# Decoding float64 weights in a fused kernel: a new order of steps, the remainder on VectorE, a third decode buffer

## The chip, the cores and the metric

One core of a Trainium2 chip runs the whole program. The metric is device time of one execution in microseconds (us), lower is better. Engines are named as the profile names them: PE is TensorE's matmuls, PEld its weight loads, DVE is VectorE, ACT ScalarE, POOL GpSimd, SP SyncE, whose queue issues most transfers. Each engine runs its own instructions strictly in the order in which the program emits them, and waits on semaphores for the others.

## The reference

Three parts, each feeding the next: a recurrent linear attention, a mixture of 8 experts with one expert per token, and a gated MLP over the 1536 tokens. The last part, with weights of 384 x 1536, 384 x 1536 and 1536 x 384, is what the diff is about:

```python
def _moe2_ref(x, w_gate, w_val, w_out) -> np.ndarray:
    gate = 1.0 / (1.0 + np.exp(-(x @ w_gate)))
    val = x @ w_val
    return (gate * val @ w_out).astype(np.float32)
...
h = np.maximum(np.einsum('ecd,edf->ecf', disp, w1), 0.0)
y = np.einsum('ecf,efd->ecd', h, w2)
```

The gated MLP's weights reach the kernel as float64 numbers (1536 x 384 of them in each of three matrices).

## The kernel before, in words

**Split products.** Every operand of a product is kept as a pair: a rounded part (`fp32r`) and the remainder that the rounding leaves. A product of two pairs is three matmuls: high by high, and the two cross terms. So each weight tile of 128 x 768 needs a copy that rounds it (ScalarE) and a subtraction that leaves the remainder (VectorE or GpSimd).

**Decoding.** The MLP's weights come as 18 tiles of 128 x 768 float64, read as pairs of 32-bit integers (`r64`, 768 KB a tile, two buffers). `decode(n)` returns a list of steps for tile n. Step o1 (L157) makes a float32 exponent and mantissa from the high word on ScalarE with Abs and a scale, into a work tile `wf`; o2 (L160) clamps it, o3 (L163) shifts it, o4 (L167) puts in the sign and o5 (L171) the low bits, all on VectorE; o6 rounds it into its home on ScalarE (L177) and subtracts on GpSimd (L178) for the remainder; o7 fetches the tile that comes two later in `ORDER` (L149), into the `r64` buffer that o5 has just read for the last time. Tiles 0 to 11 hold the gate and value weights of one block f of 128 columns each, tiles 12 to 17 the output weights of two blocks.

**Where decoding stands.** The first EARLY = 7 tiles of `ORDER` are decoded while the experts run: the expert loop has 64 iterations and 4 more, each with 9 matmuls of the first layer (`s1`), 9 of the second (`s2`, four iterations behind), and pieces of other work emitted behind them. Among these are `bg` (it rounds and subtracts one weight tile of the experts: copy L137, subtraction L139 on VectorE in even iterations and on GpSimd in odd ones, and a `raw` load on SP's queue 8 tiles ahead, which waits for its buffer), scatters of token ids by GpSimd (L190, iterations 4 to 15), `eload` (the load of an expert's tokens into `xr`, L795, in iteration f = 5 of the expert two before; TensorE transposes it at L804 in f = 1 and f = 4 of the expert before), and from iteration 6 on one step of decoding per iteration. So a tile takes seven iterations: the six steps with work, and o7.

**The MLP.** The tokens are four strips j of 384. For a strip and a block f, `mf` makes two tiles `pg` in PSUM (gate and value, 18 matmuls), `gate` makes of them the sigmoid `sg` (ScalarE), the product `gg` (VectorE), its rounded part `gh` (ScalarE) and the remainder `gl` (VectorE), and `mo` multiplies that with the output weights (9 matmuls). Two lanes of strips alternate, the second SKEW = 2 behind; `pg` is one buffer each, so the next `mf` needs `sg` done for its first half and `gg` for its second, while a `mo` of an older gate runs between two `mf`. The other 11 tiles are decoded here, one tile in each k of the loop, steps o1 to o3 ahead of the first lane's gate, o4 and o5 behind its `mo`, o6 and o7 behind the second lane.

**What sets the order.** It is written out by hand: the order of emission is the order on each engine. The lines touched are `ORDER`, `decode`, the list `dops` of the early tiles, the MLP's loop over k, and two allocations that make room for the third `wf`. The emission in the MLP's loop, shortened:

```python
for k in range(24 + SKEW):
    ops = decode(todo.pop(0)) if todo else []
    ...                                    # ops[:3]
    gate(*lane(0, k), mf(*lane(0, k)))
    mo(*lane(0, k - 1))
    ...                                    # ops[3:5]
    gate(*lane(1, b), mf(*lane(1, b)))     # b = k - SKEW
    mo(*lane(1, b - 1))
    ...                                    # ops[5:]
```

Of the kernel before, what the change touches and what calls it, by code (L numbers as in the profile page):

```python
# [7 lines left out]
F32 = mybir.dt.float32  # L8
F32R = mybir.dt.float32r
BF16 = mybir.dt.bfloat16  # L10
I32 = mybir.dt.int32
# [22 lines left out]
WARM = 16  # L34
BG = (0, 0, 0, 0, 0, 0, 4, 3)
DP = 2
ORDER = (0, 1, 2, 12, 3, 4, 13, 5, 6, 14, 7, 8, 15, 9, 10, 16, 11, 17)
EARLY = 7
HPB = 4
OVP = 60  # L40
# [62 lines left out]
def body(tc, A, out):  # L103
    nc = tc.nc
    E = mybir.EngineType
    with ExitStack() as top, tc.manual_schedule():
        gp_ = top.enter_context(tc.tile_pool(name="gp", bufs=1))
# [36 lines left out]
        r64, wyh, wyl = {}, {}, {}  # L144
        spl, homes = [None], []

        def dfetch(n):
            r64[n] = spl[0].tile([128, 768, 2], I32, tag="r64", name="r64", bufs=2)
            nc.sync.dma_start(out=r64[n].rearrange("p a b -> p (a b)"), in_=wy[n])  # L149

        def decode(n):
            t = {}

            def o1():
                t["a"] = spl[0].tile([128, 768], F32, tag="wf", name="wf", bufs=2)
                t["i"] = t["a"].bitcast(I32)
                nc.scalar.activation(out=t["a"], in_=r64[n][:, :, 1].bitcast(F32), func=AF.Abs, scale=2.0 ** 16)  # L157

            def o2():
                nc.vector.tensor_scalar(out=t["a"], in0=t["a"], scalar1=2.0, scalar2=DMAX, op0=ALU.max, op1=ALU.min)  # L160

            def o3():
                nc.vector.tensor_scalar(out=t["i"], in0=t["i"], scalar1=4, scalar2=1, op0=ALU.logical_shift_left,  # L163
                                        op1=ALU.logical_shift_right)

            def o4():
                nc.vector.scalar_tensor_tensor(out=t["i"], in0=r64[n][:, :, 1], scalar=-2 ** 31, in1=t["i"],  # L167
                                               op0=ALU.bitwise_and, op1=ALU.bitwise_or)

            def o5():  # L170
                nc.vector.scalar_tensor_tensor(out=t["i"], in0=r64[n][:, :, 0], scalar=29, in1=t["i"],  # L171
                                               op0=ALU.logical_shift_right, op1=ALU.bitwise_or)
                r64.pop(n)

            def o6():
                wyh[n], wyl[n] = homes.pop(0)
                nc.scalar.copy(out=wyh[n], in_=t["a"])  # L177
                nc.gpsimd.tensor_sub(wyl[n], t["a"], wyh[n].bitcast(F32))  # L178

            def o7():  # L180
                k = ORDER.index(n)
                if k + 2 < 18:
                    dfetch(ORDER[k + 2])

            return [o1, o2, o3, o4, o5, o6, o7]

        scx, sci = [], []

# [14 lines left out]


        rt = top.enter_context(tc.tile_pool(name="rt", bufs=2))
        tri = gp_.tile([128, 128], BF16, tag="tri", name="tri")
        ones = gp_.tile([128, 128], BF16, tag="ones", name="ones")
        warm = gp_.tile([1, 8], F32, tag="warm", name="warm")
        capi = gp_.tile([128, 1], I32, tag="capi", name="capi")
# [11 lines left out]
        with ExitStack() as ctx:  # L221
            xp_ = ctx.enter_context(tc.tile_pool(name="xsp", bufs=2))
            cp = ctx.enter_context(tc.tile_pool(name="ac", bufs=1))
# [5 lines left out]
            urow = cat[:, 128:512]  # L229
            rev = cat[:, 768:776]  # L230
            iw = cat[:, 776:1320].rearrange("p (a x) -> p a x", x=136)
            wd = cp.tile([112, 4], F32, tag="wd", name="wd")
            pw = cp.tile([112, 8, 3, 4], F32, tag="pw", name="pw")
            ft = cp.tile([112, 2, 4, 128], F32, tag="ft", name="ft")
# [459 lines left out]
        with ExitStack() as ctx:  # L694
# [18 lines left out]
            def overflow():  # L713
                with tc.If(offv["most"] > 256):
                    if True:
                        tb = rt.tile([1, 4, 40], F32, tag="tb", name="tb", bufs=1)
                        ti = rt.tile([1, 4, 40], I32, tag="ti", name="ti", bufs=1)
                        nb = cf[0:1, :].unsqueeze(2).to_broadcast([1, 8, 5])
                        ob = off[0:1, :].unsqueeze(2).to_broadcast([1, 8, 5])

                        def row(q):
                            return tb[:, q, :].rearrange("o (e j) -> o e j", j=5)

                        def con(q):
                            return cst[0:1, 128 + 40 * q:168 + 40 * q].rearrange("o (e j) -> o e j", j=5)

                        nc.vector.tensor_sub(row(0), nb, con(0))
                        nc.vector.tensor_scalar_add(row(1), nb, -256.0)
                        nc.vector.tensor_tensor(out=row(1), in0=row(1), in1=con(0), op=ALU.min)
                        nc.vector.tensor_add(row(2), row(1), ob)  # L730
                        nc.vector.tensor_add(row(1), row(1), con(1))
                        nc.vector.tensor_copy(out=row(3), in_=con(2))
                        nc.vector.tensor_scalar_max(tb, tb, 0.0)
                        nc.vector.tensor_copy(out=ti, in_=tb)
                        with tc.For_i(0, 40, 1) as i:
                            more = nc.values_load(ti[0:1, 0, bass.ds(i, 1)], min_val=0, max_val=1536,
                                                  skip_runtime_bounds_check_because="at most every token")
                            with tc.If(more > 0):
                                r0 = nc.values_load(ti[0:1, 1, bass.ds(i, 1)], engines=[E.SP], min_val=0,
                                                    max_val=8 * 1536 - 256,  # L740
                                                    skip_runtime_bounds_check_because="inside an expert's rows")
                                c0 = nc.values_load(ti[0:1, 2, bass.ds(i, 1)], engines=[E.DVE], min_val=0,
                                                    max_val=1536,
                                                    skip_runtime_bounds_check_because="inside the tokens")
                                w0 = nc.values_load(ti[0:1, 3, bass.ds(i, 1)], engines=[E.SP], min_val=0,
                                                    max_val=28,
                                                    skip_runtime_bounds_check_because="four times an expert's index")
                                block(r0, c0, w0)
# [44 lines left out]
            def eload(e, eng=nc.sync):  # L793
                xr[e] = mp.tile([128, 2, 384], F32, tag="xr", name="xr")
                after(eng.dma_start(out=xr[e], in_=xs_d[e * 1536:e * 1536 + 256, :].rearrange("(b p) d -> p b d", p=128)), scx)  # L795
# [59 lines left out]
                nc.vector.tensor_sub(XL[m][:, d], ys[e][m], XH[m][:, d].bitcast(F32))  # L855

            xt[0] = (xeh, xel)
            dops = [op for n in ORDER[:EARLY] for op in decode(n)]
            dops.reverse()
            fetch(sum(BG) + FIRST)  # L860
            eload(1)
            dfetch(ORDER[0])
            dfetch(ORDER[1])
            seq = [(e, f) for e in range(8) for f in range(8)]
# [47 lines left out]
        with ExitStack() as ctx:  # L912
# [26 lines left out]
            def gate(j, f, pg):  # L939
                sg = qp.tile([128, 384], F32, tag="sg", name="sg")  # L940
                nc.scalar.activation(out=sg, in_=pg[0], func=AF.Sigmoid)  # L941
                gg = qp.tile([128, 384], F32, tag="gg", name="gg")
                nc.vector.tensor_mul(gg, sg, pg[1])  # L943
                gh = qp.tile([128, 384], F32R, tag="gh", name="gh", bufs=7)
                gl = qp.tile([128, 384], F32R, tag="gl", name="gl", bufs=7)
                nc.scalar.copy(out=gh, in_=gg)  # L946
                nc.vector.tensor_sub(gl, gg, gh.bitcast(F32))  # L947
                gs[(j, f)] = (gh, gl)
# [21 lines left out]
            def lane(first, k):  # L970
                return (first + 2 * (k // 12), k % 12)

            todo = list(ORDER[EARLY:])
            for k in range(24 + SKEW):
                ops = decode(todo.pop(0)) if todo else []
                for op in ops[:3]:
                    op()
                if k < 24:
                    gate(*lane(0, k), mf(*lane(0, k)))
                if 0 < k <= 24:  # L980
                    mo(*lane(0, k - 1))
                for op in ops[3:5]:
                    op()
                b = k - SKEW
                if b >= 0:
                    gate(*lane(1, b), mf(*lane(1, b)))
                if 0 < b <= 23:
                    mo(*lane(1, b - 1), (0, 1, 2) if b < 20 else (0, 1) if b < 22 else (0,))
                for op in ops[5:]:
                    op()  # L990
            for f, t in ((7, 2), (8, 2), (9, 2), (9, 1), (11, 0), (10, 1), (11, 1), (10, 2), (11, 2)):
                mo(3, f, (t,))

# [16 lines left out]
```

## Time and profile before

| | |
|---|---|
| three runs | 479.15, 480.61, 486.78 us; median 480.61 |
| profiled execution | 480.61 us, of which the span of its instructions is 478.9 us |
| mean granted clock of TensorE | 0.977 |
| PE busy | 446.5 us, 93% of the span |
| DVE, ACT, POOL busy | 280.6, 220.8, 184.5 us |
| first matmul of the MLP | 241.62 us from the span's start |

The profile shows one execution. Times in its views count from the start of the span. A matmul's end is modelled, so successive matmuls overlap in it. "x <- y L9" after an idle time names what ended it and the line that issued that. The granted clock is 1.00 at 2.4 GHz and 0.50 at 1.2 GHz; a value between is a stretch with both.

### The profile page before, as it was taken

What the parts mean: (1) busy time and instruction counts of PE and PEld (TensorE: products, weight loads), DVE (VectorE), ACT (ScalarE), POOL (GpSimd) and SP (SyncE); (2) the same over time, 40 slices, a digit from 0 to 9 for tenths busy, and PEclk for the clock granted to TensorE, in tenths of its full rate; (3) what the DMA queues carried; (4) which work ended last, traced back from release to release, by engine and by line L of the source; (5) the groups of instructions that cost most, each with busy time, mean ns of one, the idle gap of its engine ahead of it and who ended that gap; (6) DMA issues with size and microseconds to landing.
All of it is one profiled execution on the core that took longest, in us unless ns stands there. A gap on an engine that the chain in (4) does not pass through costs nothing.

```text
span 478.9 us, 8621 instructions
## 1 busy us (share of the span) xinstructions
PE 446.5 (93%) x3354; PEld 431.4 (90%) x3356; DVE 280.6 (59%) x474; ACT 220.8 (46%) x450; POOL 184.5 (39%) x127
## 2 busy tenths in 40 slices
PE   6978988599979999999989899999999999999995
PEld 2777987599979999999979799999999999999995
DVE  4797997668778788889347676566222221212221
ACT  2676877536736777675332433433232322222231
POOL 4876938735885647467111311221120200000022
PEclk9979999799989999999999999999999999999999
DMA  7999951779898787773012312310010100000011
GB/s 213 347 340 309 273 203 72 248 288 216 197 227 305 269 271 238 254 258 101 3 47 86 133 66 75 124 68 0 1 49 1 49 1 0 1 1 0 1 50 49
DMA packets 23707, 65.10 MB, mean 136 GB/s; under 512 B 4592, under 2 KB 8816, under 8 KB 23664
## 3 DMA queue, kind: packets, MB, share of 16 engines
q1 hardware_dynamic: 21600, 59.80, 40.5%
q0 software_dynamic: 1920, 4.73, 2.7%
q8 instruction: 27, 0.44, 0.4%
q14 instruction: 16, 0.13, 0.1%
q10 hardware_dynamic: 144, 0.00, 0.0%
HBM read 56.65 MB, written 7.87 MB: 135 GB/s over the span
## 4 chain that ended last, share of the span: by engine, by line
PE 44%; DVE 3%; issue 3%; ACT 1%; POOL 1%; POOLq 0%; DVEq 0%; ACTq 0%
PE pg L936 28%; PE po L960 5%; PE po L959 5%; PE po L958 5%; DVE wf L160 1%; PE ph L825 1%; PE py L848 1%; DVE gg L943 1%; POOL out_dram L190 1%; PE py L849 1%; PE py L850 1%; DVE wf L167 1%; ACT wf L157 1%; DVE wf L171 0%; DVE gl L947 0%
## 5 line engine op out<-in xcount | busy, mean ns | idle before, releaser
L943 DVE TENSOR_TENSOR gg<-sg,pg 128x384 f32<-128x384 f32 x48 | 26.5, 553 | 93.6 <-PE pg L936 91.6
L139 POOL TENSOR_TENSOR rl<-raw,rh 128x768 fp32r<-128x768 f32 x26 | 52.1, 2006 | 36.0 <-ACT rh L137 35.9
L936 PE MATMUL pg<-xhi,ws 128*128 128x384 f32 x240 | 61.6, 337 | 4.6 <-ACT sg L941 3.0
L946 ACT CAST gh<-gg 128x384 fp32r<-128x384 f32 x48 | 24.7, 514 | 83.9 <-DVE gg L943 83.9
L190 POOL DMA_INDIRECT out_dram<-ob,ids x12 | 11.7, 976 | 123.8 <-ACT ob L967 121.4
L941 ACT ACTIVATE sg<-pg 128x384 f32<-128x384 f32 x48 | 23.5, 490 | 70.6 <-PE pg L936 70.6
L848 PE MATMUL py<-hh,rh 128*128 128x256 f32 x192 | 54.6, 284 | 0.0
L137 ACT CAST rh<-raw 128x768 fp32r<-128x768 f32 x64 | 51.4, 836 | 4.7 <-PE py L849 1.9
L849 PE MATMUL py<-hl,rh 128*128 128x256 f32 x192 | 53.5, 279 | 0.0
L850 PE MATMUL py<-hh,rl 128*128 128x256 f32 x192 | 53.5, 278 | 0.0
L139 DVE TENSOR_TENSOR rl<-raw,rh 128x768 fp32r<-128x768 f32 x31 | 46.3, 1497 | 10.6 <-ACT rh L137 10.5
L936 PE MATMUL pg<-xlo,rh 128*128 128x384 f32 x144 | 48.7, 338 | 0.0
L936 PE MATMUL pg<-xhi,rh 128*128 128x384 f32 x144 | 48.6, 338 | 0.0
L936 PEld LDWEIGHTS pg<-xhi,ws 128*128 128x128 f32 x240 | 43.0, 188 | 6.1 <-ACT sg L941 3.7
L936 PE MATMUL pg<-xhi,rl 128*128 128x384 f32 x144 | 48.5, 337 | 0.0
L947 DVE TENSOR_TENSOR gl<-gg,gh 128x384 fp32r<-128x384 f32 x48 | 26.8, 558 | 27.8 <-ACT gh L946 27.8
L936 PE MATMUL pg<-xlo,ws 128*128 128x384 f32 x120 | 40.2, 335 | 0.0
L178 POOL TENSOR_TENSOR rl<-wf,rh 128x768 fp32r<-128x768 f32 x8 | 14.7, 1840 | 65.4 <-ACT rh L177 59.9
L848 PEld LDWEIGHTS py<-hh,rh 128*128 128x128 f32 x192 | 36.4, 189 | 0.1
L850 PEld LDWEIGHTS py<-hh,rl 128*128 128x128 f32 x192 | 36.5, 190 | 0.0
L849 PEld LDWEIGHTS py<-hl,rh 128*128 128x128 f32 x192 | 36.5, 190 | 0.0
L327 ACT ACTIVATE at<-cst,dl 128x128 f32<-128x128 f32 x96 | 28.9, 387 | 7.6 <-DVE dl L319 7.5
(187 smaller groups left out, 1211.9 us busy)
## 6 DMA issues: line engine op xcount, KB each, us to landing
raw<-in_wx_dram SPq DMA_DIRECT2D x64, 384.0 KB, 5.6
r<-in_wy_dram SPq DMA_DIRECT2D x18, 768.0 KB, 4.5
dm<-in_dm_dram SPq DMA_DIRECT2D x8, 672.0 KB, 11.6
kr<-in_kr_dram SPq DMA_DIRECT2D x8, 576.0 KB, 11.6
v<-in_v_dram SPq DMA_DIRECT2D x8, 384.0 KB, 10.9
xs_d<-zero SPq DMA_DIRECT2D x8, 384.0 KB, 10.5
xr<-xs_d SPq DMA_DIRECT2D x8, 384.0 KB, 4.1
cat<-in_cax_dram SPq DMA_DIRECT2D x1, 404.0 KB, 13.8
```

Source lines behind the costliest of these rows:

```text
L137: nc.scalar.copy(out=h, in_=t)
L139: (nc.gpsimd if pool else nc.vector).tensor_sub(rl[n % NR], t, h.bitcast(F32))
L327: nc.scalar.mul(AT[s][:, j, :], ident, dl[:, j:j + 1])
L848: nc.tensor.matmul(y, wh[:, w], hh, start=(f == 0 and m != 1), stop=False, skip_group_check=True)
L849: nc.tensor.matmul(y, wh[:, w], hl, start=False, stop=False, skip_group_check=True)
L850: nc.tensor.matmul(y, wl[:, w], hh, start=False, stop=(f == 7), skip_group_check=True)
L936: nc.tensor.matmul(pg[g], a[:, w], b[kt][:, c], start=(kt == n == 0), stop=(kt == last and n == 2))
L943: nc.vector.tensor_mul(gg, sg, pg[1])
L946: nc.scalar.copy(out=gh, in_=gg)
L947: nc.vector.tensor_sub(gl, gg, gh.bitcast(F32))
L958: nc.tensor.matmul(po[j][t], gh[:, a], wh[:, w], start=(f == 0), stop=False)
L959: nc.tensor.matmul(po[j][t], gh[:, a], wl[:, w], start=False, stop=False)
```

## The change

Two parts of the decoding change. In `decode`, o6 only rounds, and a new step o8 subtracts on VectorE; the work tile `wf` has three buffers. In the early tiles the fetch o7 comes ahead of o6, and o6 and o8 are emitted together in the seventh iteration. In the MLP, tiles are decoded in pairs, each pair over three groups of steps; one group is emitted behind each gate of either lane (the first lane's behind its `mo`). Within a group only a step with its input from an earlier group or from no VectorE step stands on ScalarE. Output tile 14 comes one place earlier in `ORDER`, and so do 15 and 16. To make room, `tri` goes to a pool of the attention and `ti` shares memory with `tb`.

```diff
@@ -34,7 +34,7 @@
 WARM = 16
 BG = (0, 0, 0, 0, 0, 0, 4, 3)
 DP = 2
-ORDER = (0, 1, 2, 12, 3, 4, 13, 5, 6, 14, 7, 8, 15, 9, 10, 16, 11, 17)
+ORDER = (0, 1, 2, 12, 3, 4, 13, 5, 14, 6, 7, 15, 8, 9, 16, 10, 11, 17)
 EARLY = 7
 HPB = 4
 OVP = 60
@@ -152,7 +152,7 @@
             t = {}
 
             def o1():
-                t["a"] = spl[0].tile([128, 768], F32, tag="wf", name="wf", bufs=2)
+                t["a"] = spl[0].tile([128, 768], F32, tag="wf", name="wf", bufs=3)
                 t["i"] = t["a"].bitcast(I32)
                 nc.scalar.activation(out=t["a"], in_=r64[n][:, :, 1].bitcast(F32), func=AF.Abs, scale=2.0 ** 16)
 
@@ -175,14 +175,16 @@
             def o6():
                 wyh[n], wyl[n] = homes.pop(0)
                 nc.scalar.copy(out=wyh[n], in_=t["a"])
-                nc.gpsimd.tensor_sub(wyl[n], t["a"], wyh[n].bitcast(F32))
+
+            def o8():
+                nc.vector.tensor_sub(wyl[n], t["a"], wyh[n].bitcast(F32))
 
             def o7():
                 k = ORDER.index(n)
                 if k + 2 < 18:
                     dfetch(ORDER[k + 2])
 
-            return [o1, o2, o3, o4, o5, o6, o7]
+            return [o1, o2, o3, o4, o5, o6, o7, o8]
 
         scx, sci = [], []
 
@@ -203,7 +205,6 @@
 
 
         rt = top.enter_context(tc.tile_pool(name="rt", bufs=2))
-        tri = gp_.tile([128, 128], BF16, tag="tri", name="tri")
         ones = gp_.tile([128, 128], BF16, tag="ones", name="ones")
         warm = gp_.tile([1, 8], F32, tag="warm", name="warm")
         capi = gp_.tile([128, 1], I32, tag="capi", name="capi")
@@ -229,6 +230,7 @@
             urow = cat[:, 128:512]
             rev = cat[:, 768:776]
             iw = cat[:, 776:1320].rearrange("p (a x) -> p a x", x=136)
+            tri = cp.tile([128, 128], BF16, tag="tri", name="tri")
             wd = cp.tile([112, 4], F32, tag="wd", name="wd")
             pw = cp.tile([112, 8, 3, 4], F32, tag="pw", name="pw")
             ft = cp.tile([112, 2, 4, 128], F32, tag="ft", name="ft")
@@ -714,7 +716,7 @@
                 with tc.If(offv["most"] > 256):
                     if True:
                         tb = rt.tile([1, 4, 40], F32, tag="tb", name="tb", bufs=1)
-                        ti = rt.tile([1, 4, 40], I32, tag="ti", name="ti", bufs=1)
+                        ti = tb.bitcast(I32)
                         nb = cf[0:1, :].unsqueeze(2).to_broadcast([1, 8, 5])
                         ob = off[0:1, :].unsqueeze(2).to_broadcast([1, 8, 5])
 
@@ -855,7 +857,10 @@
                 nc.vector.tensor_sub(XL[m][:, d], ys[e][m], XH[m][:, d].bitcast(F32))
 
             xt[0] = (xeh, xel)
-            dops = [op for n in ORDER[:EARLY] for op in decode(n)]
+            dops = []
+            for n in ORDER[:EARLY]:
+                d = decode(n)
+                dops += [d[0], d[1], d[2], d[3], d[4], d[6], lambda d=d: (d[5](), d[7]())]
             dops.reverse()
             fetch(sum(BG) + FIRST)
             eload(1)
@@ -970,24 +975,35 @@
             def lane(first, k):
                 return (first + 2 * (k // 12), k % 12)
 
-            todo = list(ORDER[EARLY:])
+            def groups():
+                work = [decode(n) for n in ORDER[EARLY:]]
+                a, b = None, None
+                for i in range(0, len(work) + 2, 2):
+                    n, m = (work[j] if j < len(work) else [lambda: None] * 8 for j in (i, i + 1))
+                    yield [n[0]] + ([b[5], a[7]] if a else []) + [n[1], n[2]] + ([b[7]] if a else [])
+                    yield [m[0], n[3], n[4], n[6], m[1]]
+                    yield [n[5], m[2], m[3], m[4], m[6]]
+                    a, b = n, m
+
+            todo = list(groups())
+
+            def some():
+                for op in todo.pop(0) if todo else []:
+                    op()
+
             for k in range(24 + SKEW):
-                ops = decode(todo.pop(0)) if todo else []
-                for op in ops[:3]:
-                    op()
                 if k < 24:
                     gate(*lane(0, k), mf(*lane(0, k)))
                 if 0 < k <= 24:
                     mo(*lane(0, k - 1))
-                for op in ops[3:5]:
-                    op()
+                if k < 24:
+                    some()
                 b = k - SKEW
                 if b >= 0:
                     gate(*lane(1, b), mf(*lane(1, b)))
+                    some()
                 if 0 < b <= 23:
                     mo(*lane(1, b - 1), (0, 1, 2) if b < 20 else (0, 1) if b < 22 else (0,))
-                for op in ops[5:]:
-                    op()
             for f, t in ((7, 2), (8, 2), (9, 2), (9, 1), (11, 0), (10, 1), (11, 1), (10, 2), (11, 2)):
                 mo(3, f, (t,))
 
```

## Rows read from the trace of the kernel before

**Rows 1.** Waits of TensorE (PE), whole span: who released; us in total, times, longest.

```profile
PE xp L804 <- DMA xr<-xs_d: 3.5, 2, 3.2
PE pg L936 <- ACT sg L941: 3.0, 2, 2.0
...
PE pg L936 <- DVE gg L943: 0.7, 2, 0.4
```

**Rows 2.** Timeline of TensorE: start, length, work, in brackets the idle time before it.

```profile
135.66 0.52 PE L804 MATMUL xp<-cst,xr 128*128 128x128 f32 x3 [3.20 <-DMA xr<-xs_d]
...
250.76 0.62 PE L936 MATMUL pg<-xhi,ws 128*128 128x384 f32 x2 [1.03 <-ACT sg L941]
...
266.20 0.61 PE L936 MATMUL pg<-xhi,ws 128*128 128x384 f32 x2 [1.99 <-ACT sg L941]
```

**Rows 3.** Stretches: length, busy us of each engine, granted clock, DMA share, GB/s.

```profile
135.00:140.00 5.00, 4.34 (x24) 4.37 (x25) 2.87 (x4) 2.52 (x4) 3.96 (x3) 0.66 0.77 85
139.50:220.50 81.00, 81.00 (x715) 81.00 (x715) 68.77 (x80) 54.79 (x90) 48.94 (x25) 1.00 0.78 256
...
380.00:400.00 20.00, 20.00 (x116) 20.00 (x115) 5.01 (x9) 4.25 (x9) 0.00 (x0) 1.00 0.03 11
```

**Rows 4.** Timeline of ScalarE (ACT), 245 to 251 us.

```profile
248.70 0.83 ACT L177 CAST rh<-wf 128x768 fp32r<-128x768 f32 x1 [2.49 <-DVE wf L171]
...
250.23 0.48 ACT L941 ACTIVATE sg<-pg 128x384 f32<-128x384 f32 x1
```

**Rows 5.** Timeline of VectorE (DVE), 250 us.

```profile
250.36 1.48 DVE L160 TENSOR_SCALAR wf<-wf 128x768 f32<-128x768 f32 x1 [1.70 <-ACT wf L157]
```

**Rows 6.** Timeline of GpSimd (POOL), 249 us.

```profile
249.61 1.82 POOL L178 TENSOR_TENSOR rl<-wf,rh 128x768 fp32r<-128x768 f32 x1 [17.74 <-ACT rh L177]
```

**Rows 7.** Groups by line and shape, 241 to 345 us: busy us, mean ns, idle before.

```profile
L160 DVE TENSOR_SCALAR wf<-wf 128x768 f32<-128x768 f32 x11 | 15.8, 1440 | 11.7 <-ACT wf L157 11.7
...
L947 DVE TENSOR_TENSOR gl<-gg,gh 128x384 fp32r<-128x384 f32 x21 | 11.7, 558 | 12.2 <-ACT gh L946 12.2
...
L171 DVE SCALAR_TENSOR_TENSOR wf<-r,wf 128x768 int32<-128x768 int32 x11 | 10.5, 958 | 0.4
...
L157 ACT ACTIVATE wf<-r 128x768 f32<-128x768 f32 x11 | 9.8, 895 | 0.0
...
L163 DVE TENSOR_SCALAR wf<-wf 128x768 int32<-128x768 int32 x11 | 6.2, 561 | 0.4
```

**Rows 8.** Groups by line and shape, 126 to 241 us (the experts).

```profile
L139 DVE TENSOR_TENSOR rl<-raw,rh 128x768 fp32r<-128x768 f32 x24 | 38.7, 1611 | 9.7 <-ACT rh L137 9.6
...
L178 POOL TENSOR_TENSOR ws<-wf,ws 128x768 fp32r<-128x768 f32 x7 | 16.1, 2300 | 5.3 <-ACT ws L177 3.5 <-PE py L850 1.8
...
L177 ACT CAST ws<-wf 128x768 fp32r<-128x768 f32 x6 | 5.0, 834 | 8.4 <-DVE wf L171 8.4
```

**Rows 9.** The page's DMA issues: count, KB each, median us from issue to landing.

```profile
r<-in_wy_dram SPq DMA_DIRECT2D x18, 768.0 KB, 4.5
```

**Rows 10.** Timeline of GpSimd, 123 to 130 us.

```profile
123.36 1.85 POOL L139 TENSOR_TENSOR rl<-raw,rh 128x768 fp32r<-128x768 f32 x1 [0.88 <-ACT rh L137]
125.17 2.67 POOL L178 TENSOR_TENSOR ws<-wf,ws 128x768 fp32r<-128x768 f32 x1
128.00 1.74 POOL L190 DMA_INDIRECT ids_d<-tid,cpos  x1 [0.15 <-issue]
```

**Rows 11.** Timeline of VectorE, 120 us.

```profile
120.26 0.95 DVE L171 SCALAR_TENSOR_TENSOR wf<-r,wf 128x768 int32<-128x768 int32 x1
```

**Rows 12.** Timeline of SyncE's queue (SPq), 125 to 127 us.

```profile
125.65 0.38 SPq L149 DMA_DIRECT2D r<-in_wy_dram  x1
126.13 0.38 SPq L795 DMA_DIRECT2D xr<-xs_d  x1
```

**Rows 13.** DMA issues of the stretch 119 to 127 us, columns as in rows 9.

```profile
xr<-xs_d SPq DMA_DIRECT2D x1, 384.0 KB, 9.4
ids_d<-tid,cpos POOLq DMA_INDIRECT x2, 8.4
```

## The prediction, made before the change was run

> **What bounds the kernel now.** I read the waits of TensorE first, over the whole span. Three lines of the answer lie where the diff reorders work [rows 1]: a wait for transfers into `xr`, 3.5 us in two pieces, in the experts, and two in the gated MLP, 3.0 us for `sg` and 0.7 us for `gg`, twice each. The timeline of TensorE places them: the `sg` waits are 1.03 us at 250.76 and 1.99 us at 266.20 [rows 2]; each `gg` wait follows one of them by half a gate. No other wait for a gate is in the answer, so from there to the end the gates keep up. The table by stretches then shows what a stage without waits looks like: in the expert stage TensorE is busy 81.00 of 81.00 us, with VectorE at 68.77, and late in the MLP it does 116 matmuls in 20 us, 0.172 us each, so a gate with its output step (27 matmuls) lasts about 4.7 us [rows 3]. **So a better order of decoding can win 3.7 us in the MLP, and in the expert stage only what the `xr` wait costs.**
>
> Why the MLP waits: ScalarE runs in order. At 248.70 it starts the rounding copy L177 of a tile, having stood 2.49 us for VectorE's last decoding step, then the next tile's Abs, and only at 250.23 the sigmoid of a gate whose first half had long been there: TensorE stood from 249.73, and 18 matmuls of 0.172 us before that is 246.6 [rows 2 to 4]. TensorE needs that sigmoid to free `pg`. VectorE is late too: its clamp L160 takes 1.48 us while GpSimd does the remainder of the tile before, begun at 249.61 [rows 5, 6].
>
> **The change, part by part.**
>
> *1. Decoding in the MLP, eleven tiles.* Removed from ScalarE's way: the copy behind decoding steps of the same gate. In the new order a gate is followed by at most one Abs (0.90 us) and one copy (0.83 us), whose input was finished a gate earlier [rows 7, 8]. After a gate's 18 matmuls, `gg` and `gh` take about 1.3 us with their hand-overs (an estimate from `gl`'s 0.56, of the same size); the next first half is ready 18 matmuls later, at 3.1 us, and its sigmoid is wanted only after another 18, at 6.2. Two decoding steps and a sigmoid (0.90 + 0.83 + 0.48 = 2.2 us) fit into these 4.9 us.
>
> For the first gate: ScalarE is free at 246.21 (248.70 less the 2.49), Abs to 247.1, sigmoid to 247.6 instead of 250.7. TensorE finishes its output matmuls at 249.73 (250.76 less the 1.03) and finds `sg` done; `gg`, behind two decoding steps of 0.56 us, is done near 248.9, before the second half of the next gate asks for it at 251.3. So both waits go, and by the same arithmetic the pair at 266 us. Sum of the part: **-1.03 - 1.99 - 0.7 = -3.7 us**.
>
> VectorE: the clamp falls from 1.44 to the 0.56 of its neighbour L163, since GpSimd no longer works there, and a remainder of 0.96 (as L171, of the same size) is added [rows 7]. What shows that GpSimd is the cause: the clamp that started at 250.36 ended at 251.84, 0.4 us after GpSimd's remainder ended at 251.43 [rows 5, 6]. The Trainium skill (SBUF — State Buffer, "Who interferes with whom") says that the loser of the pair of ports shared by VectorE and GpSimd waits for the whole instruction; this row agrees, and by that rule the eleven moved remainders cost VectorE 11 x 0.96 and give back 11 x 0.88 us, so nothing net.
>
> The fullest of three gates holds `gg`, `gl` (0.56 each), two clamps or shifts and two remainders, 4.15 us, and the 0.58 us in which VectorE waits for `gh`: 4.7, a whole period. The other two come to 3.6 + 0.58. Over three gates that is 13.1 of 14.0 us. A gate may fall behind by a fraction; `gg` has 2.5 us of room (the output step and half a gate, 18 matmuls, less its 0.56). Cost taken: 0; if that room were gone, one wait of 0.5 to 1 us in each third gate over 18 groups, at most 6 x 1.0 = 6 us, which would undo the part.
>
> Transfers: each tile's fetch is issued right after the step that frees its buffer, and its Abs comes two gates later, some 7 us; a fetch lands in 4.5 us [rows 9]. Cost 0. The least room for a finished tile is tile 17: its remainder is emitted one pair of gates (over 7 us) before its first matmul. Cost 0.
>
> *2. The seven early tiles, in the expert stage.* Their remainders go from GpSimd (2.30 us each) to VectorE (0.96 alone; the neighbours there average 1.61 because they collide with GpSimd) [rows 8]. VectorE has 81.0 - 68.8 = 12.2 us of room in that stretch, and GpSimd has seven operations fewer to collide with. The copy now comes one iteration after the step that it waits for, so the 8.4 us in which ScalarE stood there [rows 8] mostly go. The gain and the cost are both off TensorE's path: 0, bounds in the rivals.
>
> *3. What moves on SP's queue.* The fetch of the third decoding tile (768 KB) is issued one iteration earlier. Until now it stands behind a `raw` load that waits for GpSimd's remainder of 123.36 to 125.21; ahead of that load it can go out when its buffer's last reader ends, near 121.2 [rows 10, 11]. The load of `xr` then goes out near 125.7 instead of 126.13, and the large one 4.4 us earlier [rows 12]. On GpSimd the remainder at 125.17 (2.67 us) disappears, so the scatter of ids at 128.00 moves to about 125.4, and the next with it. This load lands 9.4 us after its issue [rows 13], at 135.5, and TensorE has waited for it since 132.46: 3.20 us [rows 2]; in the 5 us after, the granted clock is 0.66, between the two levels of 2.4 and 1.2 GHz, which is another 5 x 0.34 = 1.7 us [rows 3]. No row shows this load in the new order. Best case: landed by 132.46, -4.9 us. Worst: the two scatters, 2.6 us earlier, stand in front of it and it lands 2.6 us later after issue, at 137.7: +2.2 us. Taken: 0, since the same transfers are ahead of it in both orders, and landings of 8.4 and 9.4 us there [rows 13], against 4.5 for a fetch in the MLP [rows 9], say that the transfer engines have no idle time for the early one.
>
> The third decode buffer, the moved `tri` and the aliased `ti` issue no instruction in this run: 0.
>
> **Sum.** The profiled execution took 480.61 us (span 478.9 and 1.7 around it), which is also the median of the three runs. 480.6 - 3.7 = **476.9 us**.
>
> **Rivals.**
> A. *The `xr` load comes earlier* and its stall shrinks: the large fetch is out of its way, and 6.8 us from issue to landing would do. For it: the 4.4 us. Against: full transfer engines. Time 472.0 (all of the 4.9) to 476.
>
> B. *The `xr` load comes later.* Scatters of ids land 8.4 us after issue, as slowly as the large loads next to them [rows 13], and two of them move ahead of it. Up to 476.9 + 2.2 = 479.1. The Trainium skill (DMA: Bandwidth & Descriptors, "Queues, rings and completion order") says that a transfer's completion is signalled only after every earlier write of that DMA engine, over all its queues; by it the load's landing would wait for those two scatters, the same 479.1; no run here shows yet whether it does.
>
> C. *The change doesn't do what it says*: a new wait takes the place in the MLP, by VectorE's full third gate or a fetch that holds the Abs, and with it the next sigmoid. One or two stalls of 1 to 2 us, 478 to 480.6.
>
> D. *VectorE becomes the bound of the expert stage, slower than before.* A remainder now waits on VectorE for ScalarE's copy (0.83), and may collide with a GpSimd operation (0.96 + 1.85 for one like that at 123.36). At 3.6 us for each of the six tiles in that stretch (the seventh's is the one at 125.17), 21.8 us meet 12.2 us of room: 9.6 us late on TensorE, 476.9 + 9.6 = 486.5. It decides from 12.2 / 6 = 2.0 us per tile, and the whole is slower than before from 2.7. Against: collisions get fewer, and ScalarE's copy has usually finished.
>
> **Chances.** Forecast (476.2 to 477.6) 0.47; A 0.27; B 0.13; C 0.09; D 0.04. The range takes in A's nearly whole gain and B: 472.4 to 479.2; outside lie D, the end of A, most of C. Two per cent, about what a measurement of this kernel tells from no change, are 9.6 us: faster would need 471.0, under A's best, so 0.03; slower needs 490.2, beyond D's price and reached only with C or B on top, so 0.02; within, 0.95.
>
> **What would show it.** Part 1: no wait of TensorE for `sg` or `gg` between 242 and 345 us, ScalarE's copies without a wait on the last decoding step, the clamp at 0.56 us. Part 2: TensorE still full from 140 to 220 us and VectorE's share there near 68.8 us. Part 3: the wait at L804 and the clock in the stretch behind it; if the wait isn't 3.2 us, A or B holds. Wrong would be waits of TensorE on `hl` or `rl` in the experts (D) or on `gg` in each third gate (C).

## The result and the profile after

The changed kernel took 477.22 us (median of 4 runs, 475.53 to 478.61), the kernel before 482.63 beside it (4 runs): ratio 0.9895 [0.9848, 0.9942]. The profiled execution took 478.61 us (span 476.7). The forecast was 476.9; the stages that add up to it moved otherwise than forecast. From the two timelines (start of a stage's first matmul to end of its last):

| stage, us | before | after | difference |
|---|---|---|---|
| start to the first expert matmul | 98.07 | 96.55 | -1.5 |
| experts | 142.64 | 147.42 | **+4.8** |
| experts to MLP | 0.91 | 0.92 | 0.0 |
| MLP | 231.86 | 226.46 | **-5.4** |
| tail | 5.4 | 5.4 | 0.0 |

The first row shows no effect of the change: in the kernels below it lies between 94.1 and 99.4 us, and in a second profile of the changed kernel (e5) it is 99.36. The rows add up to 2.1 us less, where the medians fell by 5.4; the profiled execution of the changed kernel is the slowest of its four.

TensorE's waits after, whole span (us in total, times, longest), to be held against [rows 1]:

```profile
PE xp L806 <- DMA xr<-xs_d: 4.2, 2, 2.4
PE pg L941 <- DVE xlo L857: 0.9, 1, 0.9
```

No wait for `sg` or `gg` is left (that for `xlo`, 0.9 us, also stood before). ScalarE after, at the place of [rows 4] (start, length, work):

```profile
249.38 0.90 ACT L157 ACTIVATE wf<-r 128x768 f32<-128x768 f32 x1
250.19 0.47 ACT L946 ACTIVATE sg<-pg 128x384 f32<-128x384 f32 x1
```

The sigmoid follows an Abs that waited for nothing; no copy stands between. VectorE after, in the fullest of three gates, from one `gg` to the next:

```profile
260.93 0.56 DVE L948 TENSOR_TENSOR gg<-sg,pg 128x384 f32<-128x384 f32 x1 [0.56 <-PE pg L941]
262.07 0.56 DVE L952 TENSOR_TENSOR gl<-gg,gh 128x384 fp32r<-128x384 f32 x1 [0.58 <-ACT gh L951]
262.54 0.95 DVE L180 TENSOR_TENSOR rl<-wf,rh 128x768 fp32r<-128x768 f32 x1
263.41 0.55 DVE L160 TENSOR_SCALAR wf<-wf 128x768 f32<-128x768 f32 x1
264.00 0.56 DVE L163 TENSOR_SCALAR wf<-wf 128x768 int32<-128x768 int32 x1
264.47 0.95 DVE L180 TENSOR_TENSOR rl<-wf,rh 128x768 fp32r<-128x768 f32 x1
265.35 0.55 DVE L948 TENSOR_TENSOR gg<-sg,pg 128x384 f32<-128x384 f32 x1
```

VectorE works without a pause from 262.07 to the `gg` of 265.35, and TensorE waits for nothing. Groups by line and shape in the MLP after (241 to 345 us; busy us, mean ns, idle before), for [rows 7]:

```profile
L180 DVE TENSOR_TENSOR rl<-wf,rh 128x768 fp32r<-128x768 f32 x8 | 7.6, 952 | 0.0
L160 DVE TENSOR_SCALAR wf<-wf 128x768 f32<-128x768 f32 x11 | 6.1, 553 | 0.3 <-ACT wf L157 0.3
L180 DVE TENSOR_TENSOR wr<-wf,wr 128x768 fp32r<-128x768 f32 x3 | 2.9, 951 | 0.0
```

The clamp fell from 1440 to 553 ns and the eleven remainders cost 7.6 + 2.9 = 10.5 us, so clamps and remainders take 16.6 us of VectorE where the clamps alone took 15.8. The same view of the experts after (126 to 241 us), for [rows 8]:

```profile
L139 DVE TENSOR_TENSOR rl<-raw,rh 128x768 fp32r<-128x768 f32 x24 | 35.4, 1476 | 4.9 <-ACT rh L137 4.8
L180 DVE TENSOR_TENSOR ws<-wf,ws 128x768 fp32r<-128x768 f32 x7 | 9.7, 1390 | 2.5 <-ACT ws L177 2.5
L177 ACT CAST ws<-wf 128x768 fp32r<-128x768 f32 x6 | 5.0, 832 | 0.2 <-DVE wf L171 0.2
```

Stretches after, for [rows 3], with one more (length, busy us of each engine with its instructions, granted clock, DMA share, GB/s):

```profile
135.00:140.00 5.00, 4.05 (x22) 4.08 (x23) 4.05 (x5) 2.05 (x3) 1.98 (x2) 0.67 0.89 174
139.50:220.50 81.00, 81.00 (x694) 81.00 (x693) 72.37 (x86) 55.49 (x90) 35.31 (x19) 1.00 0.76 248
160.00:220.00 60.00, 60.00 (x516) 60.00 (x515) 53.99 (x67) 42.36 (x69) 26.21 (x14) 1.00 0.72 243
```

**The second line holds the surprise.** TensorE is busy for all of the 81.00 us at a granted clock of 1.00, as before, but it gets 694 matmuls done where it did 715: 116.7 ns each instead of 113.3. The busy share can't show that; the count beside it does. In the rows of single matmuls the usual distance of two starts went from 113.3 to 117.8 ns. From 160 to 220 us the kernel before did 531 where the third line has 516:

```profile
160.00:220.00 60.00, 60.00 (x531) 60.00 (x530) 51.62 (x62) 40.77 (x68) 35.23 (x18) 1.00 0.74 249
```

TensorE, SyncE's queue and GpSimd around the `xr` load, for [rows 2], [rows 12] and [rows 10]:

```profile
135.95 0.52 PE L806 MATMUL xp<-cst,xr 128*128 128x128 f32 x3 [2.41 <-DMA xr<-xs_d]
```

```profile
121.96 0.33 SPq L149 DMA_DIRECT2D r<-in_wy_dram  x1
...
126.38 0.39 SPq L797 DMA_DIRECT2D xr<-xs_d  x1
```

```profile
126.09 1.53 POOL L192 DMA_INDIRECT ids_d<-tid,cpos  x1 [0.15 <-PE py L851]
127.92 0.97 POOL L192 DMA_INDIRECT ids_d<-tid,cpos  x1 [0.30 <-issue]
```

The fetch went out 3.7 us earlier, the scatters 1.9 and 2.1 us earlier, and `xr` landed 9.6 us after its issue (135.95 - 126.38), no sooner than before.

### The profile page after: what moved, and what is told of

It reads as the page before. It is cut to its first block, busy times and chain, and to the rows that moved or that the text cites. A ratio compares the mean times of both kernels' runs of the same rounds, so it can differ in the third digit from the quotient of the medians.

```text
span 476.7 us, 8610 instructions
## 1 busy us (share of the span) xinstructions
PE 451.0 (95%) x3355; PEld 436.8 (92%) x3356; DVE 289.6 (61%) x492; ACT 222.1 (47%) x450; POOL 142.8 (30%) x109
## 4 chain that ended last, share of the span: by engine, by line
PE 48%; issue 2%; POOL 1%; POOLq 0%; ACT 0%; DVE 0%; ACTq 0%
PE pg L941 31%; PE po L964 5%; PE po L963 5%; PE po L965 5%; PE ph L827 1%; PE py L850 1%; PE py L852 1%; PE py L851 1%; POOL out_dram L192 1%; POOLq L1022 0%; ACT sg L946 0%; DVE xlo L857 0%; ACT xhi L856 0%; POOLq L192 0%; ACTq L946 0%
## 5 line engine op out<-in xcount | busy, mean ns | idle before, releaser
L139 POOL TENSOR_TENSOR rl<-raw,rh 128x768 fp32r<-128x768 f32 x26 | 50.0, 1923 | 61.5 <-ACT rh L137 61.5
L139 DVE TENSOR_TENSOR rl<-raw,rh 128x768 fp32r<-128x768 f32 x31 | 43.3, 1399 | 5.7 <-ACT rh L137 5.3
L941 PE MATMUL pg<-xlo,rh 128*128 128x384 f32 x120 | 40.2, 335 | 0.0
L941 PE MATMUL pg<-xhi,rh 128*128 128x384 f32 x120 | 40.2, 335 | 0.0
L941 PE MATMUL pg<-xhi,rl 128*128 128x384 f32 x120 | 40.1, 335 | 0.0
L835 ACT ACTIVATE hh<-ph 128x512 fp32r<-128x512 f32 (+1 forms) x33 | 19.4, 587 | 39.1 <-PE ph L827 33.2
```

Of the source, the lines that this page charges most:

```text
L139: (nc.gpsimd if pool else nc.vector).tensor_sub(rl[n % NR], t, h.bitcast(F32))
L941: nc.tensor.matmul(pg[g], a[:, w], b[kt][:, c], start=(kt == n == 0), stop=(kt == last and n == 2))
```

## The experiments

**Where the slower matmuls come from.** Only the alias of `ti` moves other tiles: it frees 640 bytes a partition in a pool, and everything allocated later starts 640 bytes lower (`tri` and the third `wf` are whole multiples of 256 bytes). In the compiled program the starts, modulo 256 bytes, were: the experts' weights `rh` 96 in both kernels; `XH` and `ws` 224 before, 96 after; `xh`, `hh` and `gh` 32 before, 160 after. Two kinds of tiles stay at 32 in both: `xeh` and `xel`, the tokens of experts 0, 2, 4 and 6 in the first layer, and `wr`, a part of the MLP's weights. The first theory was that these starts set the distance of matmuls, by the half of 256 bytes in which each operand lies; the rival was that VectorE's remainders slow TensorE in the experts.

*e1: the kernel before with the alias alone.*

```diff
-                        ti = rt.tile([1, 4, 40], I32, tag="ti", name="ti", bufs=1)
+                        ti = tb.bitcast(I32)
```

> The kernel before, with one line changed: ti shares memory with tb, so everything allocated later moves down by 640 bytes. Instruction order unchanged. Address theory (the changed kernel's matmuls in the experts start every 117.6 ns instead of 113.5 because a moving tile and a weight tile then start in different halves of a 256-byte unit): experts slower by about 4 us (117 to 118 ns for matmuls on xh and hh), the MLP's pg matmuls at 173.6 ns instead of 175, its four stalls of 3.7 us still there; total 2 to 3 us slower than before. Rival (the slower rate comes from VectorE's added remainders, or from the chip): 113.5 ns in the experts, total within 1 us of before.

485.94 us (median of 11), ratio to before 1.0054 [1.0028, 1.0079]. Stretch of e1, columns as above:

```profile
160.00:220.00 60.00, 60.00 (x517) 60.00 (x517) 50.12 (x63) 41.81 (x69) 33.47 (x18) 1.00 0.77 257
```

517 matmuls, with GpSimd still doing the early remainders. An edit that issues no instruction costs 2.6 us [1.4, 3.8] by the ratio, 1.6 by the medians; the rival fell.

*e2: the changed kernel with 64 bytes fewer in the pool ahead of the experts' tiles* (`ids` shares memory with `tid`), so that `xh`, `hh` and `gh` start at 96.

```diff
-        ids = gx.tile([128, 12], I32, tag="ids", name="ids")
+        ids = tid
```

> The changed kernel, with ids loaded into the tile tid, so r64 and everything behind it (xr, xh, xl, hh, hl, gh, gl) moves down by 64 bytes; instruction order unchanged. Address theory: all moving and weight tiles then start in the same half of a 256-byte unit: 113.5 ns in the experts (4 us less) and 173.5 ns for the output matmuls instead of 176.2 (1.1 us less), about 472 us. Rival (VectorE's work or the chip): rates as in the changed kernel, 477 us.

480.39 us, 0.9933 [0.9906, 0.9959]. Stretch of e2:

```profile
160.00:220.00 60.00, 60.00 (x511) 60.00 (x511) 53.91 (x66) 41.77 (x68) 24.98 (x14) 1.00 0.71 241
```

The MLP's output matmuls did as expected (starts 173.7 ns apart, 176 to 177 in the changed kernel), but the experts got slower still: 511 matmuls, starts 120 ns apart. **So the rule of halves fell.** What fits the kernels up to here, with exceptions, is the distance of the two operands' starts: that of the operand that moves minus that of the one loaded as weights, modulo 256. In the experts and in `mf` the tokens move; in `mo` the tokens `gh` are the ones loaded, and the output weights move. In the experts 192 goes with 113.3 ns, 64 with 117.8, 0 with 120; in the MLP, with 384 columns, 0 and 64 with 173.5, 128 and 192 with 175.5 to 177. The matmuls with `wr` fit it less well: in e2 `mo` has 174 ns there at 192.

The changed kernel holds a test of it in one stretch, where the first layer of an even expert (`xeh`, 192) gives way to the second layer (`hh`, 64):

```profile
180.92 0.28 PE L827 MATMUL ph<-xeh,rh 128*128 128x256 f32 x1
...
181.60 0.28 PE L850 MATMUL py<-hh,rh 128*128 128x256 f32 x1
...
182.31 0.28 PE L850 MATMUL py<-hh,rh 128*128 128x256 f32 x1
```

Six matmuls take 0.68 us up to 181.60 and the next six 0.71, 113 and 118 ns each; in the kernel before, both layers have 113. So in the changed kernel the even experts' first layer mostly keeps the old distance, and the mean over the stage is 116.7, not 117.8. The next three kernels test the rule further.

*e6, e7, e8: the changed kernel with a pad of 128 bytes.* In e6 it stands at the start of two pools, so that `xh`, `hh` and `gh` start at 32 again and `XH` and `ws` stay at 96; e7 is e6 with the scatters late (see e3); in e8 it stands in the pool of `tb`, so that every operand starts where it did before the change. The tile `ho` moves into a `wf` buffer for room.

```diff
+            mp.tile([128, 32], F32, tag="pad", name="pad", bufs=1)     # e6, e7
+            qp.tile([128, 32], F32, tag="pad", name="padq", bufs=1)    # e6, e7
+                        rt.tile([1, 32], F32, tag="pad", name="pad", bufs=1)    # e8
-                    ho = hp.tile([128, 256], F32, tag="ho", name="ho", bufs=1)
+                    ho = spl[0].tile([128, 768], F32, tag="wf", name="ho", bufs=3)[:, 0:256]
```

> The changed kernel, with 128 unused bytes ahead of xr, xh, hh and gh (room for it comes from ho, used only in a branch not taken here, which goes into the wf buffers). Order of instructions unchanged. From the runs so far, by the distance of the moving tile's start from the weight tile's, modulo 256 bytes: at 256 columns 192 gives 113.4 ns, 64 gives 117.7, 0 gives 120; at 384 columns 0 and 64 give 173.5, 128 and 192 give 175.5 to 177. Here the distances are 192 in the experts, 0 or 64 in the MLP: 113.4 and 173.5 everywhere, 4 us less in the experts and 1.1 us less in the MLP, 5 us less than the changed kernel. If only the half of a 256-byte unit counted, the same for this kernel. Rival (no such rule of distance): rates of 117 to 120 in the experts.

> The changed kernel, with 128 unused bytes added to the pool of ti's neighbours (and ho in the wf buffers as in e6_pad), so that every operand starts at the same place modulo 256 bytes as in the kernel before: the change without its shift. Placement theory: 113.4 ns in the experts, pg 175 and output step 173 to 177 as before, the MLP shorter by the four stalls alone (3.7 us), total 0.985 to 0.992 of before. Rival (the slower experts come from VectorE's remainders): 117 ns in the experts.

Beside them, on the same chip, the changed kernel once more (e5):

> The changed kernel as it is, on the chip of the next three. Placement theory (a matmul's rate follows from where its two operands start in SBUF): the same rates as in its first profile, 118 ns on xh and hh, 173.6 for pg, 176 for the output step; ratio to before near 0.99. Rival (the rate is a matter of the single execution or of the chip): other rates. The wait for the second xr load lies between 2 and 4 us.

e5 479.93 us, 0.9937 [0.9905, 0.9968]; e6 476.57, 0.9882 [0.9844, 0.992]; e8 475.83, 0.986 [0.9819, 0.9901]. The stretch in e5, e6 and e8:

```profile
160.00:220.00 60.00, 60.00 (x515) 60.00 (x515) 54.03 (x66) 41.76 (x68) 25.36 (x15) 1.00 0.73 245
```

```profile
160.00:220.00 60.00, 60.00 (x531) 60.00 (x530) 55.17 (x66) 42.61 (x68) 27.19 (x14) 1.00 0.72 240
```

```profile
160.00:220.00 60.00, 60.00 (x531) 60.00 (x530) 55.16 (x67) 42.92 (x70) 27.54 (x15) 1.00 0.75 252
```

With the same decoding the pads bring back 531 matmuls, the kernel before's rate. The medians fall by 3.4 and 4.1 us against e5. It isn't the whole law. In e6's MLP 173.5 ns were expected everywhere and 1.1 us less; the matmuls into `pg` are 174.4 ns apart on average, those of `mo` with `wr` (distance 0) 176, and the stage is 226.10 us, 0.4 less. And e8 ran at 117.8 ns from 146 to 157 us, e1 at 113.3 from 166 to 173: both changes in e8 and the first in e1 come right behind a transposition into `xp` (at 146.07, 157.00 and 165.47 us), and e1 changes back where the next expert's `xeh` begins. Most transpositions change nothing.

**The early tiles by themselves.** *e4: the changed kernel with the early tiles as before* (the remainder on GpSimd behind the copy, the fetch last).

```diff
+            def o9():
+                nc.gpsimd.tensor_sub(wyl[n], t["a"], wyh[n].bitcast(F32))
...
-                dops += [d[0], d[1], d[2], d[3], d[4], d[6], lambda d=d: (d[5](), d[7]())]
+                dops += [d[0], d[1], d[2], d[3], d[4], lambda d=d: (d[5](), d[8]()), d[6]]
```

> The changed kernel, with the seven early tiles decoded as before: remainder on GpSimd right behind the rounding copy, the fetch one iteration later; the MLP keeps the new order. My theory (the early part is neutral for TensorE but for the xr wait): no wait of TensorE for hl or rl, the xr wait at about 3.2 us, ScalarE again some 8 us behind the last decoding step, total within 1 us of the changed kernel. Rival (VectorE's remainders slow TensorE's matmuls in the experts): 113.5 ns there again, and 4 us less in total.

480.26 us, 0.9948 [0.992, 0.9976], against 0.9933 to 0.9937 of e2 and e5: no difference that can be told. The experts' matmuls stay 118 ns apart (x516 from 160 to 220 us), which refutes the rival a second time. The `xr` waits are 5.4 us, where 3.2 were expected.

**What holds the `xr` load.** *e3: the changed kernel with the scatters of ids put off* from iteration 4 to iteration 48.

```diff
-                    if i >= 4 and nid < 12:
+                    if i >= 48 and nid < 12:
```

> The changed kernel, with the twelve scatters of ids emitted in iterations 48 to 59 instead of 4 to 15. Scatter theory (the scatters hold the transfer engines, and the xr loads land late for it): the two waits of TensorE for xr, 4.2 us together, fall below 1 us, the half-clock stretch after the second goes (another 1.7 us), total about 4 to 6 us less than the changed kernel. Rival (the large fetch and the raw loads fill the queue, scatters cost nothing): waits of 3 to 4 us stay, total as the changed kernel.

474.06 us, 0.9807 [0.9778, 0.9836]. TensorE's waits in e3, the lines for `xp` and `pg`:

```profile
PE xp L806 <- DMA xr<-xs_d: 2.1, 1, 2.1
PE pg L941 <- DVE xlo L857: 0.9, 1, 0.9
```

The wait near 135 us is gone, and with it the stretch of lowered clock: the granted clock is 1.00 from 35.8 us nearly to the end. The other wait, at 105.30 us, stays; below 1 us was expected. e2 and e4, on the same chip with the scatters early, took 480.39 and 480.26: 6.3 and 6.2 us more.

*e7: e6 with the scatters late.*

> As e6_pad, and the scatters of ids in iterations 48 to 59 as in e3_scatter_late. If both effects are real and independent: 5 us and 4 us less than the changed kernel, about 0.97 of before, waits for xr at 2 us or less. Rival: with the faster experts the loads are later than their use again, and the xr waits eat the gain, 0.98.

**471.74 us, 0.9778 [0.9742, 0.9815], the best of all kernels here**, a little less gain than expected; 4.8 us under e6, 8.2 under the changed kernel (e5). DMA issues of e7 from 118 to 135 us (KB each, median us from issue to landing), for [rows 9] and [rows 13]:

```profile
raw<-in_wx_dram SPq DMA_DIRECT2D x8, 384.0 KB, 3.9
r<-in_wy_dram SPq DMA_DIRECT2D x1, 768.0 KB, 6.1
xr<-xs_d SPq DMA_DIRECT2D x1, 384.0 KB, 5.1
```

and the load of `xr` in e6, which differs from e7 by the scatters alone (six of them in the same stretch):

```profile
xr<-xs_d SPq DMA_DIRECT2D x1, 384.0 KB, 8.5
```

The load that took 9.4 us before and 8.5 in e6 lands in 5.1, and no wait for `xr` is left in the experts. The queue's rows rule out that GpSimd, freed of the scatters, only lets the loads go out sooner: the fetch and `xr` are issued at 122.41 and 126.83 us in e7, 121.58 and 126.02 in e6, behind the same loads. So the scatters hold the loads. Whether a load's completion waits for theirs, as the rule of the Trainium skill that rival B cites (DMA: Bandwidth & Descriptors, "Queues, rings and completion order") would have it, or they slow the transfers themselves, these runs don't tell.

**Which part of the change freed the MLP.** *e10: the changed kernel with the MLP's remainders on GpSimd; e11: the kernel before with them on VectorE.*

```diff
+                eng = nc.vector if n in ORDER[:EARLY] else nc.gpsimd     # e10, in o8
+                eng = nc.gpsimd if n in ORDER[:EARLY] else nc.vector     # e11, in o6
+                eng.tensor_sub(wyl[n], t["a"], wyh[n].bitcast(F32))
```

> The changed kernel with the remainders of the eleven MLP tiles on GpSimd again, in the new order. What removed the four waits of TensorE in the MLP? Theory 1 (the order: nothing stands on ScalarE whose input is fresh): still no wait for sg or gg; the clamp L160 in the MLP rises from 0.55 us toward 1.4 us where it collides with GpSimd, VectorE has 0.95 us less per tile to do, the MLP stays at 226.5 us and the total at the changed kernel's 477 to 480. Theory 2 (VectorE free of GpSimd is what removed them): waits for sg and gg of 1 to 4 us in all come back, MLP 228 to 230 us.

> The kernel before with only the remainders of the eleven MLP tiles moved to VectorE, in the old order. Theory 1 (the order): ScalarE's copy still stands behind decoding steps of the same gate, and VectorE now waits for that copy before its remainder, so the sg waits stay at 3.0 us or grow, and gg too; the MLP at 231 to 234 us, the total as before or up to 2 us more. Theory 2 (the engine): the clamp falls to 0.56 us, the sg and gg waits go, MLP 228.1 us, total 3.7 us less than before.

e10 took 480.43 us, 0.9936 [0.9906, 0.9966], with an MLP of 226.5 us (249.39 to 475.89). Its waits, `xp` and `pg`:

```profile
PE xp L807 <- DMA xr<-xs_d: 5.9, 1, 5.9
PE pg L942 <- DVE xlo L858: 0.9, 1, 0.9
```

and two VectorE groups of its MLP:

```profile
L167 DVE SCALAR_TENSOR_TENSOR wf<-r,wf 128x768 int32<-128x768 int32 x11 | 18.2, 1654 | 0.2
...
L160 DVE TENSOR_SCALAR wf<-wf 128x768 f32<-128x768 f32 x11 | 6.1, 557 | 1.5 <-ACT wf L157 1.5
```

All four waits are gone with the new order (and its third `wf` buffer) without the new engine. Where the collision falls was misjudged: the clamp stays at 557 ns, and the sign step L167 now takes 1654 (954 in the changed kernel). e11 took 481.13 us, 0.9963 [0.9938, 0.9988], with an MLP of 229.46 us. Its waits for gates, and ScalarE at the place of [rows 4]:

```profile
PE pg L937 <- ACT sg L942: 1.9, 2, 1.0
```

```profile
252.06 0.83 ACT L177 CAST rh<-wf 128x768 fp32r<-128x768 f32 x1 [2.48 <-DVE wf L171]
252.80 0.90 ACT L157 ACTIVATE wf<-r 128x768 f32<-128x768 f32 x1
253.59 0.48 ACT L942 ACTIVATE sg<-pg 128x384 f32<-128x384 f32 x1
```

With the old order the copy still stands 2.48 us ahead of the sigmoid, and 1.9 of 3.0 us of `sg` waits stay; the faster clamp takes off the rest and the `gg` waits. So both theories held half: the new order is enough without the engine, the engine alone does half.

## Why the prediction came out as it did

**The MLP: right in mechanism, the term too small.** All four waits went, for the reason given, and no wait came in their place; VectorE's full gate ran as worked out (from `gg` at 260.93 to `gg` at 265.35 us, 4.4 of 4.7 us forecast; over the eleven tiles the remainders cost VectorE 0.8 us more than the clamps give back, where nothing net was forecast). But the term was 3.7 us and the stage gained 5.4. A wait costs more than its listed length. The last matmul ahead of the wait of 1.03 us and the first ones behind it, TensorE before:

```profile
249.39 0.34 PE L960 MATMUL po<-ws,gl 128*128 128x384 f32 x1
...
251.40 0.51 PE L936 MATMUL pg<-xhi,ws 128*128 128x384 f32 x2
```

Without a wait the next matmul would have started 0.17 us after 249.39; it started 1.37 us after [rows 2], 1.20 late, of which the list counts only what follows the matmul's modelled end. The pair behind the wait then takes 0.62 us [rows 2] where the pair at 251.40 takes 0.51: 0.11 more. That is 1.3 us for a wait of 1.03. Over the four waits the starts are late by 4.4 us and the matmuls behind them by 0.4 more: 4.8 us for 3.7 listed. e8, which has the new order and the old places, has an MLP of 226.82: 5.04 less than before. The other 0.2 us lie in the usual distance of its matmuls, 174.8 ns on average against 175.0. The remaining 0.4 us, down to 226.46, goes with the new places of the operands.

**The early tiles: right about the time.** VectorE had the room (72.37 us of 81.00, though near 68.8 was forecast), ScalarE's wait on L171 fell from 8.4 to 0.2 us, and e4 finds no difference in time. Rival D did not come: at 1.4 us a tile it stayed under its deciding point of 2.0.

**The `xr` load: taken at 0, and nothing that can be told from 0.** Two profiles of the changed kernel have 4.2 us in two waits and 2.7 in one, before 3.5 in two; the other kernels with early scatters have 2.3 (e6) to 6.9 (e11). The fetch went out 3.7 us earlier, of 4.4 forecast, `xr` itself 0.25 later, and the load landed no sooner, so rival A's mechanism isn't seen; rival B named the right thing, the scatters, but two of them 2 us earlier made the load no later (9.6 us against 9.4). What counts is whether they are in that stretch at all (e3, e7). So the loads ahead of it, which the reason for the 0 counts on, aren't what held it: behind the same loads it landed in 5.1 us (e7).

**The step that failed** is "The third decode buffer, the moved `tri` and the aliased `ti` issue no instruction in this run: 0." The alias costs 2.6 us by itself (e1) and its undoing wins 3.4 to 4.1 (e6, e8). In the profiled experts it is 1152 matmuls of the two layers by 3.4 ns, 3.9 us, and the rest of the +4.8 is 0.7 us more of `xr` waits and what lies within such profiles' scatter.

**The total: near, and partly by luck.** The forecast had 3.7 us of gain and no loss; the profiles show 5.4 gained in the MLP and some 4 to 5 lost in the experts, so 0.6 to 1.4 in all. The medians fell by 5.4 us [2.8, 7.3], on another chip by 3.3 [1.5, 4.6] (e5); no stage that the change touches accounts for more than 1.4 of it, and executions of one kernel differ by 3 us and more (475.53 to 478.61). The forecast also started from 480.61 us, where the median before is now 482.63. That 477.22 lies 0.3 us from 476.9 says little about the terms.

What stays open: why the starts of operands matter, and why a transposition sometimes lets the distance flip for some microseconds. The third `wf` buffer wasn't tried by itself.

## What to carry to other kernels

An engine that runs in order and is wanted by the critical loop should get only side work whose inputs are a period old; that, with a third work buffer, removed all four waits here, and a listed wait of TensorE was worth about 0.3 us more than its length. When an edit moves memory, compare the count of matmuls in a stretch in which TensorE is full, not its busy share: 694 against 715 showed a loss as large as the gain aimed at, where the busy share showed none. And look at what runs beside a late load before moving the load itself: putting off small scatters won 4.8 to 6.3 us, the change 3.3 to 5.4.

## What the runs showed of the hardware

- The distance of successive matmuls depended on where their operands start in a partition: with 256 columns 113.3, 117.8 and 120 ns where the moving operand starts 192, 64 and 0 bytes (modulo 256) behind the loaded one, with 384 columns 173.5 ns at 0 and 64 against 175.5 to 177 at 128 and 192, all at a granted clock of 1.00. The half of 256 bytes in which each starts explained it less well (e2), some pairs don't fit (`wr`), and behind a transposition it can flip (e1, e8).
- Scatters of ids, six from 118 to 135 us, held a 384 KB load at 8.5 us from issue to landing (e6), and at 9.4 in the kernel before; without them it took 5.1 (e7), and the `raw` loads beside it 3.9 against 8.1.
- A wait of 2.4 us of TensorE at 135.95 us was followed by a granted clock of 0.67 in the 5 us from 135, between the two levels of 1.2 and 2.4 GHz; where that wait was gone (e3, e7), the clock stayed at 1.00 there. Not every such wait is followed by a fall: before, the 1.99 us up to 266.20 were not, in e1 the same wait was (0.66 from 274 to 279 us), and in e3 2.1 us at 105.30 were not.
- VectorE's clamp and sign step were long where GpSimd worked beside them: the clamp at 1440 ns on average before, the sign step at 1654 in e10, 553 and 954 with GpSimd idle there. In e10 a sign step that began 0.28 us after a subtraction of GpSimd took 2.50 us and ended 0.8 behind it, and one with GpSimd idle 0.95:

```profile
262.67 1.98 POOL L181 TENSOR_TENSOR rl<-wf,rh 128x768 fp32r<-128x768 f32 x1 [23.87 <-ACT rh L177]
```

```profile
262.95 2.50 DVE L167 SCALAR_TENSOR_TENSOR wf<-r,wf 128x768 int32<-128x768 int32 x1
...
271.53 0.95 DVE L167 SCALAR_TENSOR_TENSOR wf<-r,wf 128x768 int32<-128x768 int32 x1
```

The Trainium skill (SBUF — State Buffer, "Who interferes with whom") says that whichever of the two takes the ports that they share first holds them for its whole instruction, while the other stands; these numbers agree. It is not every step: `gg`, which reads one of its inputs from PSUM, took its usual 0.56 us at 269.42 in e10, inside a subtraction of GpSimd (269.08 to 271.19).
